# Attention and expert layer on one core: another order of the first quarter on all engines

## The chip, the cores and the metric

The kernel runs on one core of a Trainium2 chip. The metric is the device time of one execution, in microseconds (us). The engines work at the same time, each through its own list of instructions in order: TensorE (PE, with its weight loads PEld), VectorE (DVE), ScalarE (ACT), GpSimd (POOL), and SyncE (SP), which here only issues DMAs.

## The reference

A gated linear attention is followed by a two-layer network with a gated activation. All is float32; B = 4, H = 8 heads, S = 768 steps, D = 48, model width 384, inner width 2048.

```python
f = 1.0 / (1.0 + np.exp(-f_logit))
for t in range(S):
    state = f[:, :, t, :, None] * state + np.einsum('bhd,bhe->bhde', k[:, :, t], v[:, :, t])
    y[:, :, t] = np.einsum('bhd,bhde->bhe', q[:, :, t], state)
x = y.transpose(0, 2, 1, 3).reshape(B * S, H * D)
h = x @ w_in
g = h * np.clip(h + 3.0, 0.0, 6.0) / 6.0
out = g @ w_out
```

## The kernel before, in words

The 768 steps of each of the 4 sequences are cut into 6 chunks of 128. One chunk of one sequence is a *unit*; unit i is sequence i % 4 of chunk i // 4, so there are 24. The four units of a chunk form a *group* of 512 columns for the network, whose inner width is cut into 16 tiles f. A network step is numbered 16 x group + f, so mm1.0 to mm1.15 belong to the first group, which needs units 0 to 3.

The kernel is written as a table, ORDER, of 1,374 small steps, `op.number`, with a third number for the PSUM bank where one is used. A loop walks over the table and issues each step; every engine then gets its own steps in exactly this order, and waits at each for what it reads and for the buffers that it overwrites. Two more tables say which steps go to another engine than their usual one: ON_POOL (to GpSimd instead of VectorE) and ON_ACT (`lim` to ScalarE instead of VectorE).

Steps of a unit:

- `load`, `loadq`, `loadv` (SP): the DMAs of gate logits, of q and k, and of v. `load.i` overwrites the gates that `qmul.i-2` read.
- `gate` (ACT, L368): the sigmoid. Unit 0's is done in two halves, before and after the change.
- `back` (DVE, L375): the scan of the gates backwards; `rend` (L391) its reciprocal, `end` (ACT, L394) a copy; `fwd` (DVE, L399) the scan forwards.
- `kmul` (L388), `qmul` (L404), `decay` (L407): products with k, q and the state, on VectorE or GpSimd.
- `tk` (PE, L462) and `ktok` (ACT, L469): k turned. `kv` (PE, L481), `carry0`, `carry1` (L494 to L503): the new state.
- `att` (PE, L443), `mask` (DVE, L450), `qs` (PE, L513), `av` (PE, L530): the output of the unit, in PSUM.
- `xh` (ACT, L549) takes the output's upper part; `xl` its rest, on VectorE (L562), or, where a `ym` step has first subtracted the upper part on TensorE (L553), as a copy on ScalarE (L560). `hole` (SP, L567, two DMAs) fills the gaps of the layout. Then the unit's columns can be used by `mm1`.

The weights arrive as float64 bit patterns and are turned into a pair of float32 values per tile f: `ld` (SP, L255) loads, `z` (ACT, L278) rounds, `cy` and `lim` (L266, L270 on ACT, or `lim` alone, L272 on DVE) with `mid` (L285), `dif` (L290) and `top` (L294, all DVE) mend the exponent, `high` (ACT, L306) writes the upper part, `low` (L309, or its halves `lowi` and `lowo`) the lower. For tiles 0 to 2 `wd` (SP, L313) keeps the output weights whole.

Network steps: `mm1` (PE, L598, nine matmuls of 512 columns), `relu` (ACT, L608), `g` (DVE, L612), `gh` (ACT, L621), `gl` (DVE or GpSimd, L625), `mm2` (PE, L642). As units 2 and 3 come later than 0 and 1, tiles 0 to 2 of the first group are done in halves of 256 columns: `mm1a`, `relua`, `ga`, `mm2a` need units 0 and 1 alone, `mm1b` and so on units 2 and 3 (L664 to L683). `mm2a` needs `wd`.

`warm.n` is n matmuls on blank data into a bank that nobody reads (L821), `tiny.n` n short ones (L828). They keep TensorE occupied.

A step that writes a PSUM bank waits until every other engine's earlier step on that bank is done. So `att.1` into banks 0 and 1 waits for the steps that read unit 0's output there, and `mm1a.2`, into one of the banks of unit 3's output, waits for `xl.3`. SBUF buffers also turn: three for q and k, three for v, two for gates.

Of the kernel before, what the change touches and what calls it, by code (L numbers as in the profile page):

```python
# [66 lines left out]
loadv.5 top.4 mm2b.0 z.5 carry0.4 relub.1 mid.5 mm2a.2 mask.4 high.4 gb.1 cy.6 carry1.4 dif.5 mm2b.1 low.4 relub.2
lim.6 top.5 tk.5.0 mm1.3.3 z.6 mid.6 fwd.5 mm1.4.4 dif.6 qmul.5 relu.3 gb.2 end.5 high.5 g.3 decay.5 gate.6 low.5
att.5.2 ktok.5 mm2b.2 relu.4 back.6 top.6 qs.4.0 kmul.6 av.4 loadq.7 g.4 high.6 loadv.6 mask.5 loadv.7 mm1.5.4 gh.3
ld.12 lim.7 gh.4 load.7 low.6 ld.11 xh.4 gl.4 ld.15 gl.3 mm2.3 relu.5 rend.6 z.7 g.5 mid.7 z.8 lim.8 mm2.4 dif.7 gh.5  # L70
top.7 z.9 mid.8 mm1.6.2 high.7 dif.8 cy.9 low.7 end.6 top.8 kv.5.0 decay.6 relu.6 tk.6.4 lim.9 mm1.7.3 carry0.5 xl.4
gl.5 cy.10 mid.9 high.8 fwd.6 qs.5.0 relu.7 av.5 dif.9 qmul.6 mm2.5 xh.5 loadv.8 carry1.5 g.7 loadq.8 ktok.6 g.6 z.10
low.8 ym.5 lim.10 mm1.8.4 top.9 gate.7 gh.6 back.7 high.9 att.6.2 mid.10 gh.7 kv.6.0 kmul.7 gl.6 mm2.6 cy.11 rend.7
mask.6 lim.11 dif.10 z.11 low.9 tk.7.2 mm1.9.3 top.10 ktok.7 relu.8 fwd.7 high.10 end.7 relu.9 low.10 gl.7 mm2.7 g.8
carry0.6 gh.8 mm1.10.4 g.9 cy.12 carry1.6 qmul.7 xl.5 mid.11 load.9 gl.8 lim.12 mm2.8 ld.13 decay.7 hole.5 dif.11 gh.9
mid.12 z.12 dif.12 qs.6.2 top.11 att.7.0 loadq.9 top.12 av.6 high.11 load.8 kv.7.0 relu.10 gl.9 mm2.9 low.11 xh.6
carry0.7 mask.7 z.14 g.10 gate.9 qs.7.0 xl.6 z.13 lim.13 av.7 hole.6 mid.13 mm1.11.2 xh.7 lim.14 gh.10 loadv.9 dif.13
hole.4 mid.14 high.12 gl.10 mm2.10 top.13 relu.11 gate.8 g.11 low.12 gh.11 mm1.12.3 high.13 gl.11 carry1.7 xl.7 low.13
hole.7 mm1.13.4 dif.14 loadq.10 top.14 mm2.11 back.8 high.14 relu.12 low.14 kmul.8 z.15 mm1.14.1 lim.15 relu.13 g.12
g.13 mid.15 mm1.16.0 gh.13 dif.15 top.15 gl.13 tk.8.2 high.15 mm2.13 end.8 gh.12 low.15 relu.14 rend.8 gl.12 mm1.15.4  # L80
fwd.8 qmul.8 mm2.12 back.9 relu.15 load.10 relu.16 g.15 ktok.8 g.14 att.8.2 g.16 kv.8.2 gh.14 mm1.17.4 mask.8 gl.14
rend.9 gate.10 fwd.9 gh.15 mm2.14 gl.15 qmul.9 back.10 mm2.15 lowo.0 mm1.19.1 outs.0 outv.1 kmul.9 end.9 gh.16 outs.2
gl.16 decay.8 relu.17 mm1.18.0 od.2 rend.10 load.11 relu.19 g.17 od.0 carry0.8 fwd.10 mm2.16 relu.18 g.19 end.10
qmul.10 carry1.8 g.18 tk.9.3 kmul.10 load.12 lowo.1 mm1.20.4 loadv.10 ktok.9 od.1 gh.17 decay.9 gh.18 gl.17 gate.11
qs.8.0 back.11 att.9.2 decay.10 loadq.11 av.8 kv.9.2 gl.18 xh.8 mm2.17 gate.12 carry0.9 carry1.9 lowo.2 end.11 mask.9
mm1.21.2 gh.19 gl.19 xl.8 tk.10.3 relu.21 mm2.18 ktok.10 g.21 relu.20 rend.11 back.12 qs.9.0 gh.21 fwd.11 att.10.2
# [879 lines left out]
```

## Time and profile before

| | us |
|---|---|
| median of 3 runs | 467.57 (466.38 to 467.74) |
| the profiled execution | 467.04 |
| its span, first to last instruction | 465.3 |
| busy: PE, DVE, ACT, POOL | 453.9, 289.9, 212.3, 63.6 |

A profile row names line, engine, operation, output and inputs, with start and length in us. A part in brackets at its end is the idle time of the engine just before it, and what ended that. In tables of stretches "x" counts instructions; the last three columns are the granted TensorE clock, the DMA engines' busy share and GB/s.

### The profile page before, as it was taken

What the parts mean: (1) busy time and instruction counts of PE and PEld (TensorE: products, weight loads), DVE (VectorE), ACT (ScalarE), POOL (GpSimd) and SP (SyncE); (2) the same over time, 40 slices, a digit from 0 to 9 for tenths busy, and PEclk for the clock granted to TensorE, in tenths of its full rate; (3) what the DMA queues carried; (4) which work ended last, traced back from release to release, by engine and by line L of the source; (5) the groups of instructions that cost most, each with busy time, mean ns of one, the idle gap of its engine ahead of it and who ended that gap; (6) DMA issues with size and microseconds to landing.
All of it is one profiled execution on the core that took longest, in us unless ns stands there. A gap on an engine that the chain in (4) does not pass through costs nothing.

```text
span 465.3 us, 11483 instructions
## 1 busy us (share of the span) xinstructions
PE 453.9 (98%) x4967; PEld 387.4 (83%) x4967; DVE 289.9 (62%) x455; ACT 212.3 (46%) x365; POOL 63.6 (14%) x65
## 2 busy tenths in 40 slices
...
DMA packets 19113, 44.91 MB, mean 97 GB/s; under 512 B 2544, under 2 KB 8816, under 8 KB 19056
## 3 DMA queue, kind: packets, MB, share of 16 engines
...
q8 instruction: 41, 0.67, 0.6%
q10 hardware_dynamic: 288, 0.26, 0.2%
q14 instruction: 16, 0.13, 0.1%
...
## 4 chain that ended last, share of the span: by engine, by line
PE 89%; DVE 3%; ACT 3%; DMA 2%; issue 1%; SPq 0%; POOL 0%; ACTq 0%; POOLq 0%
PE o L642 34%; PE pair L598 25%; PE single L598 12%; PE pair L513 3%; PE pair L530 2%; PE pair L443 2%; PE o L683 2%; PE idle L821 2%; PE pair L481 2%; DMA v<-unit 1%; PE pair L698 1%; PE single L698 1%; PE pair L462 1%; PE pair L664 1%; DVE gg L625 1%
## 5 line engine op out<-in xcount | busy, mean ns | idle before, releaser
L642 PE MATMUL o<-gg,weight 128*128 128x512 f32 x693 | 162.6, 383 | 0.4 <-DVE gg L625 0.3
L642 PEld LDWEIGHTS o<-gg,weight 128*128 128x128 f32 x693 | 129.1, 189 | 19.3 <-DVE gg L625 1.6
L598 PE MATMUL pair<-xts,weight 128*128 128x512 f32 x576 | 133.1, 381 | 0.4 <-DVE tg L612 0.4
L598 PEld LDWEIGHTS pair<-xts,weight 128*128 128x128 f32 x576 | 107.7, 189 | 15.4 <-DVE tg L612 0.8
L625 DVE TENSOR_TENSOR gg<-tg,gg 128x512 fp32r<-128x512 f32 x73 | 54.6, 752 | 56.1 <-ACT gg L621 55.9
L612 DVE SCALAR_TENSOR_TENSOR tg<-tg,pair 128x512 f32<-128x512 f32 x64 | 43.4, 683 | 55.7 <-ACT tg L608 55.5
L608 ACT ACTIVATE tg<-pair,half 128x512 f32<-128x512 f32 x64 | 43.5, 684 | 73.7 <-PE pair L598 68.5
L621 ACT ACTIVATE gg<-tg 128x512 fp32r<-128x512 f32 x77 | 47.7, 627 | 63.9 <-PE o L642 51.1
L598 PE MATMUL single<-xts,weight 128*128 128x512 f32 x261 | 61.9, 382 | 0.0
L598 PEld LDWEIGHTS single<-xts,weight 128*128 128x128 f32 x261 | 48.6, 189 | 6.9 <-DVE tg L612 0.2
L608 ACT ACTIVATE tg<-single,half 128x512 f32<-128x512 f32 x29 | 19.8, 684 | 32.8 <-PE single L598 29.2
L375 DVE TENSOR_TENSOR_SCAN suffix<-gates,unit 112x516 f32<-112x516 f32 (+1 forms) x25 | 29.4, 1180 | 3.4 <-ACT gates L368 3.4
L399 DVE TENSOR_TENSOR_SCAN gates<-gates,rend 112x516 f32<-112x516 f32 x24 | 30.2, 1260 | 0.3
L388 POOL TENSOR_TENSOR qkf<-qkf,suffix 112x512 f32<-112x512 f32 x14 | 20.8, 1483 | 65.9 <-DVE suffix L375 23.1
L612 DVE SCALAR_TENSOR_TENSOR tg<-tg,single 128x512 f32<-128x512 f32 x29 | 19.8, 682 | 9.7 <-ACT tg L608 9.4
L549 ACT ACTIVATE xts<-pair 112x512 fp32r<-112x512 f32 x24 | 14.2, 593 | 24.1 <-PE pair L530 19.4
L407 POOL TENSOR_TENSOR decayed<-state,ends 112x192 f32<-112x192 f32 x13 | 10.2, 786 | 108.6 <-PE pair L513 65.4
L404 POOL TENSOR_TENSOR qkf<-qkf,gates 112x512 f32<-112x512 f32 x11 | 15.8, 1436 | 67.4 <-DVE gates L399 39.3
L642 PE MATMUL o<-xts,weight 128*128 128x512 f32 x96 | 23.4, 380 | 0.0
L450 DVE TENSOR_TENSOR a<-pair,causal 128x512 f32<-128x512 f32 x24 | 16.4, 683 | 8.5 <-PE pair L481 5.3
L625 DVE TENSOR_TENSOR xts<-tg,xts 128x512 fp32r<-128x512 f32 x16 | 10.9, 691 | 15.4 <-ACT xts L621 15.4
L642 PEld LDWEIGHTS o<-xts,weight 128*128 128x128 f32 x96 | 17.6, 190 | 2.3
...
## 6 DMA issues: line engine op xcount, KB each, us to landing
...
xts<-xts SPq DMA_DIRECT2D x48, 48.0 KB, 2.2
weight<-w SPq DMA_DIRECT2D x3, 192.0 KB, 5.1
...
```

Source lines behind the costliest of these rows:

```text
L375: nc.vector.tensor_tensor_scan(flat(sf[:, p])[:, ::-1], gt[:, columns(p)][:, ::-1], flat(unit[:, p])[:, ::-1], 0.0, op0=ALU.mult, op1=ALU.add,
L388: engine("kmul", i).tensor_tensor(parts_of(t, 1), parts_of(t, 1), split(sf[:, :, 1:C + 1]), op=ALU.mult)
L399: nc.vector.tensor_tensor_scan(past, past, flat(rend), 0.0, op0=ALU.mult, op1=ALU.add)
L404: engine("qmul", i).tensor_tensor(parts_of(t, 0), parts_of(t, 0), split(to), op=ALU.mult)
L450: nc.vector.tensor_tensor(d["a"].rearrange("r p e t -> r e p t"), d["at"], causal.unsqueeze(1).unsqueeze(1).broadcast_to([128, 2, NP, HC]) ...
L549: nc.scalar.activation(parts(0), d["y"][:PR], AF.Copy)
L598: nc.tensor.matmul(h, win(f, a, k), turned(g["xt"][:, k, :g["n"] // C, b]), start=i == 0, stop=i == 3 * KT - 1,)
L608: nc.scalar.activation(d["t"], d["h"], AF.Relu, bias=half, scale=1.0 / 6.0)
L612: nc.vector.scalar_tensor_tensor(d["t"], d["t"], 1.0, d["h"], op0=ALU.min, op1=ALU.mult)
L621: nc.scalar.activation(d["gg"][:, 0], d["t"], AF.Copy)
L625: engine("gl", g["first"] + f).tensor_tensor(d["gg"][:, 1], d["t"], d["gg"][:, 0].bitcast(F32), op=ALU.subtract)
L642: nc.tensor.matmul(g["o"][m], wout(f, a, m), halves_of(g[f]["gg"][:, b]), start=f == 0 and i == 0, stop=f == NF - 1 and i == 2, skip_group ...
```

## The change

Only the three tables change. Every engine's list is another one up to about a quarter of the work; from there the lists agree but for a few neighbours. No step's code changes. What the tables say, from the start:

- TensorE: the warm-ups ahead of `tk.0` go from 17 and 8 tiny ones to 14 and 5; over all, from 44 and 8 to 47 and 5 by count of the table. `qs.0` goes ahead of `tk.1`. `ym.0` and `ym.2` are dropped, so `xl.0` and `xl.2` move from ScalarE to VectorE. `mm1a.0` now stands ahead of `kv.3` and `att.3`, `mm1a.1` behind `mm2a.0`, and `att.4`, `kv.4` behind the halves.
- ScalarE: `gate.1` moves behind `ktok.0`; tile 2 is converted ahead of tile 1; `lim.6` and `cy.6` go, `lim.7` and `cy.7` come.
- GpSimd, 48 to 44 steps: `kmul.3`, `kmul.4`, `qmul.5`, `decay.5`, `gl.5`, `gl.14`, `kmul.10` go to VectorE; `qmul.3`, `low.6`, `lowo.1` come from it.
- SP: `loadv.1` behind `load.2`; `ld.2` ahead of `ld.1`; `hole.0`, `hole.1` with `ld.3` ahead of `load.4`, `loadv.3`, `wd.0`, `ld.4`; then `wd.2`, `hole.2`, `ld.5`, `wd.1`, `loadv.4`, `hole.3`.

The core of the diff:

```diff
 ON_POOL = """
-kmul.1 kmul.3 lowi.0 lowi.1 kmul.4 decay.4 kmul.5 qmul.5 decay.5 kmul.6 gl.4 decay.6 gl.5 qmul.6 kmul.7 low.10 low.11
-gl.11 kmul.8 gl.14 qmul.9 lowo.0 kmul.9 decay.8 qmul.10 kmul.10 decay.9 decay.10 lowo.2 kmul.12 decay.12 qmul.13
+kmul.1 lowi.0 qmul.3 lowi.1 decay.4 kmul.5 low.6 gl.4 kmul.6 decay.6 qmul.6 kmul.7 low.10 low.11 gl.11 kmul.8 qmul.9
+lowo.0 kmul.9 decay.8 qmul.10 decay.9 lowo.1 decay.10 lowo.2 kmul.12 decay.12 qmul.13 qmul.14 qmul.15 kmul.15 decay.15
...
 ON_ACT = """
-lim.1 lim.2 lim.4 lim.5 lim.6 lim.9 lim.10 lim.11 lim.12
+lim.2 lim.1 lim.4 lim.5 lim.7 lim.9 lim.10 lim.11 lim.12
 """.split()
 ORDER = """
-load.0 warm.17 tiny.8 loadq.0 load.1 loadv.0 loadv.1 loadq.1 ld.0 gate.0 back.0 rend.0 kmul.0 gate.1 fwd.0 tk.0.0
-end.0 warm.1 ktok.0 qmul.0 kv.0.0 back.1 load.2 att.0.2 carry0.0 ld.1 warm.1 loadq.2 rend.1 kmul.1 mask.0 fwd.1 tk.1.4
-qs.0.0 lim.0 av.0 qmul.1 gate.2 warm.2 end.1 mid.0 ktok.1 load.3 back.2 loadq.3 carry1.0 kv.1.2 xh.0 loadv.2 z.0 ld.2
-warm.9 rend.2 dif.0 loadv.3 fwd.2 cy.1 lim.1 top.0 ym.0 att.1.2 mid.1 gate.3 kmul.2 carry1.1 end.2 qmul.2 xl.0 tk.2.4
-warm.2 carry0.1 mask.1 high.0 wd.0 qs.1.0 back.3 av.1 loadq.4 hole.0 att.2.2 xh.1 dif.1 kmul.3 warm.4 z.1 xl.1 load.4
-mask.2 ktok.2 hole.1 lowi.0 cy.2 rend.3 top.1 tk.3.4 warm.2 ld.3 kv.2.2 ktok.3 lim.2 kv.3.0 fwd.3 carry0.2 z.2 warm.2
-mid.2 qs.2.2 qmul.3 warm.2 carry1.3 dif.2 load.5 att.3.0 gate.4 ld.4 top.2 av.2 high.1 wd.1 mm1a.0.4 loadv.4 carry0.3
-mask.3 lowi.1 end.3 carry1.2 loadq.5 xh.2 back.4 warm.1 high.2 ym.2 qs.3.0 relua.0 av.3 lowi.2 xl.2 kmul.4 lim.3
-warm.1 xh.3 hole.2 mm1a.1.2 ga.0 end.4 xl.3 mm2a.0 relua.1 hole.3 decay.4 gate.5 ga.1 mid.3 z.3 rend.4 mm1a.2.1 dif.3
...
+load.0 warm.14 tiny.5 loadq.0 load.1 loadv.0 loadq.1 ld.0 gate.0 back.0 rend.0 end.0 kmul.0 fwd.0 tk.0.4 warm.3 ktok.0
+gate.1 qmul.0 kv.0.0 back.1 load.2 att.0.2 carry1.0 loadv.1 carry0.0 warm.2 ld.2 rend.1 kmul.1 qs.0.0 loadq.2 mask.0
+fwd.1 tk.1.2 av.0 ktok.1 lim.0 warm.11 xh.0 mid.0 gate.2 qmul.1 z.0 xl.0 load.3 loadv.2 back.2 ld.1 kv.1.2 hole.0
+dif.0 cy.2 att.1.0 top.0 warm.2 loadq.3 lim.2 ld.3 mask.1 end.1 carry0.1 rend.2 z.2 kmul.2 qs.1.0 fwd.2 tk.2.4 gate.3
+warm.2 ktok.2 av.1 qmul.2 warm.4 xh.1 back.3 high.0 att.2.2 cy.1 xl.1 lowi.0 mask.2 hole.1 kv.2.0 lim.1 mid.2 rend.3
+dif.2 carry0.2 load.4 carry1.1 warm.1 qs.2.0 top.2 z.1 loadv.3 wd.0 av.2 mid.1 ld.4 kmul.3 warm.2 xh.2 loadq.4 dif.1 tk.3.3
+fwd.3 mm1a.0.4 ktok.3 high.2 wd.2 top.1 qmul.3 warm.1 xl.2 high.1 kv.3.2 lowi.2 hole.2 relua.0 warm.1 lowi.1 att.3.0
+carry0.3 lim.3 gate.4 warm.2 ga.0 ld.5 end.2 carry1.3 mask.3 wd.1 qs.3.2 cy.4 back.4 loadv.4 av.3 lim.4 warm.2 mid.3
+mm2a.0 kmul.4 end.4 xh.3 decay.4 z.3 xl.3 dif.3 hole.3 mm1a.2.2 z.4 rend.4 mid.4 dif.4 tk.4.3 load.5 relua.2 mm1a.1.4
...
```

47 lines of the change are left out of this document (23 added, 24 removed).

## The prediction

> **What bounds the kernel now.** I read the head of the page first, then a table of stretches, then the chain that ended last, then the rows of each engine in the first 80 us.
>
> ```profile
> PE 453.9 (98%) x4967; PEld 387.4 (83%) x4967; DVE 289.9 (62%) x455; ACT 212.3 (46%) x365; POOL 63.6 (14%) x65
> ```
>
> TensorE is busy for 98% of the span of 465.3, so time can only come from its idle time, its warm-ups, or work that is dropped. Stretch by stretch (length, then busy time of each engine, clock, DMA share):
>
> ```profile
> 3.88:27.62 23.74, 20.75 (x526) 13.08 (x524) 21.98 (x33) 15.81 (x32) 4.16 (x4) 1.00 0.98 339
> 27.62:55.87 28.25, 26.75 (x340) 22.68 (x338) 26.15 (x41) 21.95 (x37) 7.61 (x8) 1.00 0.86 323
> 55.87:77.86 21.99, 21.60 (x249) 17.53 (x247) 21.34 (x33) 21.16 (x29) 7.59 (x6) 1.00 0.49 176
> 110.00:465.30 355.30, 350.04 (x3468) 306.01 (x3467) 188.38 (x298) 130.25 (x233) 34.96 (x29) 1.00 0.18 56
> ```
>
> Until 77.86 us VectorE is as full as TensorE: it idles 1.76, 2.10 and 0.65 us, 4.51 us in all. After 110 us it is busy for 53% and TensorE for 99%: there the order of the small steps decides nothing. The chain shows the hand-over (start, length, what):
>
> ```profile
> 29.84 0.69 PE pair L530 x32
> ...
> 53.82 2.23 PE single L598 x9
> ...
> 56.66 0.87 ACT w L278
> ...
> 71.63 1.60 DVE gg L625
> ...
> 77.92 0.92 PE o L642 x3
> ```
>
> Up to mm1.5 (53.82) the chain is TensorE's; then ScalarE's roundings and VectorE's conversions carry it to gl.7 (ends 77.86); from mm2.7 on it is TensorE's to the end. So the change is worth what it moves two points by: mm1.5 on TensorE, gl.7 on VectorE; the later one counts.
>
> ```profile
> 1.07 5.96 PE L821 MATMUL idle<-blank 128*128 128x512 bf16 x17 [1.07 <-DVE blank L218]
> ...
> 7.07 0.58 PE L462 MATMUL pair<-ident,qkf 112*128 112x112 f32 x4
> ...
> 13.61 2.12 PE L821 MATMUL idle<-blank 128*128 128x512 bf16 x9
> ...
> 33.02 0.38 PE L664 MATMUL pair<-xts,weight 128*128 128x256 f32 x1 [1.28 <-issue]
> 33.23 1.46 PE L683 MATMUL o<-th,weight 128*128 128x256 f32 x6
> ...
> 37.95 1.27 PE L664 MATMUL single<-xts,weight 128*128 128x256 f32 x9
> 39.05 1.17 PE L664 MATMUL pair<-xts,weight 128*128 128x256 f32 x9
> ...
> 73.28 0.92 PE L642 MATMUL o<-gg,weight 128*128 128x512 f32 x3 [0.28 <-DVE gg L625]
> ```
>
> The first output matmul, mm2a.0, starts at 33.23; a half mm1 takes 1.10 (37.95 to 39.05). A warm-up at the full clock takes 0.22 (nine in 2.12, the end of the last apart); the first 17 take 5.96 as the clock is low at the start.
>
> **The change, part by part.** Step lengths on VectorE are differences of starts in this stretch, in which no GpSimd instruction runs:
>
> ```profile
> 7.81 1.23 DVE L375 TENSOR_TENSOR_SCAN suffix<-gates,unit 112x516 f32<-112x516 f32 x1
> ...
> 11.50 0.54 DVE L272 TENSOR_SCALAR y<-raw 128x768 int16<-128x768 int16 x1
> 11.95 0.69 DVE L404 TENSOR_TENSOR qkf<-qkf,gates 112x512 f32<-112x512 f32 x1
> 12.55 0.35 DVE L285 TENSOR_SCALAR t<-y 128x768 int16<-128x768 int16 x1
> 12.82 1.23 DVE L375 TENSOR_TENSOR_SCAN suffix<-gates,unit 112x516 f32<-112x516 f32 x1
> 14.08 0.18 DVE L391 RECIPROCAL rend<-suffix 112x4 f32<-112x4 f32 x1
> 14.18 0.53 DVE L290 TENSOR_TENSOR y<-y,t 128x768 int16<-128x768 int16 x1
> 14.62 1.22 DVE L399 TENSOR_TENSOR_SCAN gates<-gates,rend 112x516 f32<-112x516 f32 x1
> 15.77 1.02 DVE L294 SCALAR_TENSOR_TENSOR w<-y,w 128x768 int16<-128x768 int16 x1
> 16.69 0.33 DVE L285 TENSOR_SCALAR t<-y 128x768 uint16<-128x768 uint16 x1
> 16.95 0.67 DVE L388 TENSOR_TENSOR qkf<-qkf,suffix 112x512 f32<-112x512 f32 x1
> 17.55 0.67 DVE L404 TENSOR_TENSOR qkf<-qkf,gates 112x512 f32<-112x512 f32 x1
> 18.16 0.67 DVE L450 TENSOR_TENSOR a<-pair,causal 128x512 f32<-128x512 f32 x1
> ...
> 33.94 0.42 DVE L678 SCALAR_TENSOR_TENSOR th<-th,pair 128x256 f32<-128x256 f32 x1 [1.38 <-ACT th L673]
> ...
> 71.54 1.69 DVE L625 TENSOR_TENSOR gg<-tg,gg 128x512 fp32r<-128x512 f32 x1
> ```
>
> lim 0.45, a whole 512-wide product or difference (kmul, qmul, mask, xl, gl) 0.60, mid 0.27, back 1.26 (1.14 without the wait for its end), rend 0.10, dif 0.44, fwd 1.15, top 0.92; lowi 0.45 and ga 0.33 by their widths.
>
> *Head.* The warm-ups ahead of tk.0 go from 17 and 8 tiny ones to 14 and 5. The three fall away at the full clock, so tk.0 starts 0.7 earlier than 7.07, at 6.35; kmul.0, two steps ahead of back.1, is done by then. gate.1 moves behind ktok.0 on ScalarE:
>
> ```profile
> 6.54 0.63 ACT L368 ACTIVATE gates<-gates 112x512 f32<-112x512 f32 x1 [2.39 <-DMA gates<-unit]
> ...
> 7.69 0.54 ACT L469 ACTIVATE ktok<-pair 128x448 f32<-128x448 f32 x1 [0.42 <-PE pair L462]
> ```
>
> ktok.0 comes at 6.95, gate.1 at 7.4, so back.1 starts at 8.0 instead of 7.81, 0.2 late; without the earlier tk.0 it would be 0.9. On VectorE then back.1, rend.1, mask.0, fwd.1, lim.0, mid.0, qmul.1, xl.0: 4.91 from 8.0, and 0.6 for fwd.1 behind kmul.1 on GpSimd (below): 13.5. xl.0 is then done, and the ym.0 of before is gone.
>
> *To the first output matmul.* VectorE's list goes on with back.2 to kmul.3: back twice and fwd once (3.67), two dif and two top (2.72), two mid (0.54), rend twice (0.20), six products (3.60): 10.7, kmul.3 done at 24.2. That releases tk.3 and mm1a.0. Then dif.1, fwd.3, top.1, xl.2, lowi.2, lim.3, ga.0, mask.3: 4.94, mask.3 done at 29.1, or 29.7 if the two GpSimd steps beside it (qmul.3, lowi.1) block 0.3 each; I take 29.5. av.3 (0.69, the row at 29.84), two warm-ups (0.43) and the latencies between (0.2) put mm2a.0 at 30.8. The queue of SP now has hole.1 ahead of load.4, loadv.3, wd.0 and ld.4, and hole.1 waits for xl.1 (done at 21.0). Issue to landing:
>
> ```profile
> xts<-xts SPq DMA_DIRECT2D x48, 48.0 KB, 2.2
> weight<-w SPq DMA_DIRECT2D x3, 192.0 KB, 5.1
> ```
>
> wd.0 leaves behind five DMA issues (hole.1 is two) of about 0.5 each, at 23.5, and lands at 28.6, needed at 30.8: covered by 2.2. hole.1 lands at 24.3 in a quiet queue; at wd.0's 5.1 it lands at 27.2 and mm1a.0 slips by 2.6, of which the wait for mask.3 covers all but the ga.0 behind it.
>
> Before, mm1a.1 was already done at mm2a.0; now it isn't. The lead is 33.23 - 30.8 - 1.10 = 1.3 us. From there to mm1.5 the same pieces run in another order, with one new wait: mm1a.2 takes the banks that xl.3 still reads, 0.1 to 0.3. Lead at mm1.5: 1.1.
>
> *What VectorE carries.* Up to gl.7 it gains kmul.3, kmul.4, qmul.5, gl.5, xl.0, xl.2 (0.60 each), decay.5 (0.27) and lim.6 (0.45), 4.32; it loses qmul.3 (0.60), low.6 (0.87, twice lowi's work less its fixed part) and lim.7 (0.45), 1.92. Net 2.4 us more. Against that stand three GpSimd steps fewer in the stretch. What one costs VectorE:
>
> ```profile
> 71.46 1.22 POOL L388 TENSOR_TENSOR qkf<-qkf,suffix 112x512 f32<-112x512 f32 x1 [3.73 <-DVE suffix L375]
> ...
> 77.13 2.43 POOL L309 TENSOR_TENSOR weight<-w,weight 128x768 fp32r<-128x768 f32 x1 [4.45 <-ACT weight L306]
> ```
> ```profile
> L272 DVE TENSOR_SCALAR y<-raw 128x768 int16<-128x768 int16 x7 | 6.6, 937 | 0.0
> ```
>
> gl.6 (71.54) took 1.69 where such a step, product or difference, takes 0.67: it ended 0.6 after kmul.7 on GpSimd did. The lim steps average 0.94 against 0.54 alone. But beside low.10 (77.13, 2.43 long) no step of VectorE was stretched. So between 0 and 1.0 per GpSimd step; I take 0.3, as most rows are unstretched: 0.9 back for three. This agrees in kind with the Trainium skill, "SBUF — State Buffer", "Who interferes with whom": a VectorE instruction with two SBUF inputs and a GpSimd one that reads SBUF lock each other out, and the second to start waits for the whole of the first. By that rule alone three steps of 1.3 would give back up to 3.9 where I take 0.9, and low.6, moved to GpSimd, could take 2.4 of it: gl.7 up to 3.0 earlier or 1.5 later than in my sum, which goes by the 0.3 of the rows.
>
> gl.7 then comes at 77.86 + 2.4 - 0.9 less the idle time saved. Against the 4.51 idle my walk has 0.2 (back.1), 0.6 (fwd.1 behind kmul.1) and 0.5 (ga.2, behind mm1a.2): 3.2 saved, gl.7 at 76.2, 1.7 early. ScalarE loses the copies of xl.0 and xl.2 and is not the limit.
>
> *The sum.* TensorE leads by 1.1 at mm1.5. In 55.87 to 77.86 it idled 0.39, and mm2.6's wait (0.28 at 73.28) belongs to it; with VectorE 1.7 ahead these go: 1.5. The ym.0 and ym.2 that are dropped lay in time that warm-ups filled, nothing. Later swaps (gl.14, kmul.10 to VectorE, lowo.1 to GpSimd) lie where VectorE idles half the time, nothing. The profiled execution took 467.04, 0.5 under the median of the runs, 467.57; 1.5 off its own time is 465.5, off the median 466.1, which is my forecast.
>
> **The rivals.**
> - *VectorE's extra work decides (slower).* If its idle time up to gl.7 stays at 4.5 and the blocking is what it was, gl.7 comes 2.4 later and all behind it: 470.0. It ends slower by 0.3% when idle time and blocking together give back less than 1.0 of the 2.4. For it: VectorE is 97% busy in 55.87 to 77.86. Against: 1.38 of the idle (33.94) is the late mm1a.1, gone by the new order.
> - *The lead is given back (no change).* The 1.28 at 33.02 has no releaser in the trace, so it is in the program before and in none of my steps; if one like it falls between av.3 and mm2a.0, the lead is gone: 467.3.
> - *More.* If neither fwd.1 (0.6) nor the list up to mask.3 (0.4) is blocked, mm2a.0 starts at 29.8, the lead is 33.23 - 29.8 - 1.10 = 2.3, and with the 0.4 of waits at the other end 2.7: 464.9. For it: most rows beside a GpSimd step are unstretched. Against: gl.6 and the mean of lim.
> - *The clock drops.* Three fewer early warm-ups, and a wait for kmul.3 before tk.3. Before, a wait of 1.28 left the granted clock at 1.00. At the start it took some 4.4 us to come up (5.96 less seven warm-ups of 0.22, an estimate); as long at half clock costs 2.2, which makes of the forecast 468.3 and without its gain 469.8. The Trainium skill, "TensorE: Matmul & The Clock Gate", "What's actually happening", gives about 3.4 us of idleness for that; nothing here is near it.
>
> **How the numbers follow.** A difference of 0.3%, 1.4 us, is what a measurement here can tell. The forecast, a gain of 1.0 to 2.2 (465.4 to 466.6), has 0.45, of which 0.35 lies beyond 1.4; the lead given back 0.26; more 0.12; VectorE's extra work 0.14, of which 0.03 within 1.4; the clock 0.03, of which 0.01 within. Faster 0.47, same 0.40, slower 0.13. The range from 463.8 to 468.4 leaves out most of the two slower cases (0.13) and the far end of the gains (0.05).
>
> **What would show it.** Right: tk.0 at 6.35, back.1 at 8.0, mm1a.0 near 24.5, mm2a.0 near 30.8, VectorE's idle between back.0 and gl.7 under 2 us, gl.7 near 76.2, and TensorE without the gap in mm2.6. Wrong: hole.1 landing after 26, a gap without releaser ahead of mm2a.0, VectorE steps of 1 us and more beside qmul.3 and low.6, or TensorE idle behind gl.6 and gl.7 as before.

## The result and the profile after

The changed kernel takes 472.78 us (median of 12 runs, 467.88 to 474.32), the kernel before beside it 467.64 (12 runs, 466.28 to 469.61): a ratio of 1.0097, 95% interval 1.0075 to 1.0119. The change made the kernel 5.1 us slower; 466.1 was forecast, with 468.4 as the upper end. The profiled execution took 472.71 with a span of 470.9, 5.6 over the span before, so the two profiles hold the whole difference of the medians.

Lines of after.py are one less than those of the kernel before (L642 is now L641). First the busy times of the page and its chain by engine; the chain of the kernel before stands as the third row.

```profile
PE 456.1 (97%) x4963; PEld 386.4 (82%) x4963; DVE 296.6 (63%) x461; ACT 211.5 (45%) x363; POOL 59.2 (13%) x61
PE 75%; DVE 11%; DMA 8%; ACT 3%; SPq 1%; issue 1%; DVEq 0%; ACTq 0%
```
```profile
PE 89%; DVE 3%; ACT 3%; DMA 2%; issue 1%; SPq 0%; POOL 0%; ACTq 0%; POOLq 0%
```

TensorE lost its place in the chain to DMAs (2% to 8%) and VectorE (3% to 11%). The same stretches as in the prediction, of the changed kernel, and the stretch to 110 us of the kernel before:

```profile
3.88:27.62 23.74, 20.18 (x446) 12.48 (x445) 21.42 (x33) 14.14 (x26) 2.19 (x2) 0.93 0.84 298
27.62:55.87 28.25, 25.30 (x317) 20.70 (x315) 25.44 (x40) 20.16 (x37) 4.95 (x4) 1.00 0.90 315
55.87:77.86 21.99, 21.84 (x335) 17.22 (x333) 21.85 (x36) 20.12 (x29) 8.94 (x6) 1.00 0.64 242
77.86:110.00 32.14, 30.35 (x317) 24.81 (x315) 30.78 (x46) 21.94 (x34) 7.67 (x4) 1.00 0.27 85
```
```profile
77.86:110.00 32.14, 31.99 (x383) 27.10 (x384) 31.39 (x51) 21.05 (x32) 7.05 (x4) 1.00 0.33 102
```

Three things changed. In the first stretch the clock is 0.93 instead of 1.00 and the DMA share 0.84 instead of 0.98. In the second, VectorE is busy for 0.7 us less although it has more to do: it waits. In the last, where I had put nothing, TensorE is idle for 1.79 us instead of 0.15.

Event by event: gl.7 starts at 80.33 instead of 77.20, 3.1 late; gl.9 ends at 90.35 instead of 85.33, 5.0 late; behind that 0.6 is added, and after 110 us nothing. TensorE's rows (start, length; in brackets the wait and what ended it):

```profile
17.80 0.46 PE L512 MATMUL pair<-qkf,middle 48*64 48x64 f32 x16 [1.86 <-ACT middle L493]
18.19 0.98 PE L461 MATMUL single<-ident,qkf 112*128 112x112 f32 x4
...
19.96 1.13 PE L529 MATMUL pair<-a,v 64*64 64x64 f32 x32
...
34.03 1.56 PE L682 MATMUL o<-th,weight 128*128 128x256 f32 x6
37.02 1.27 PE L663 MATMUL pair<-xts,weight 128*128 128x256 f32 x9 [1.42 <-DVE xts L561]
...
90.41 0.92 PE L641 MATMUL o<-gg,weight 128*128 128x512 f32 x3 [1.20 <-DVE gg L624]
```

*ScalarE's list.* qs.1 (17.80) waits 1.86 us for carry0.1 on ScalarE, and mm1a.2 (37.02) 1.42 for xl.3. Both times ScalarE sat in front of a weight conversion whose DMA had not landed, with the unit's step behind it (for xl.3 there is a second wait, that of kmul.4, below):

```profile
15.42 0.99 ACT L265 ACTIVATE y<-raw,lowest 128x768 uint16<-128x768 int16 x1 [1.77 <-DMA raw<-w]
16.50 0.94 ACT L269 ACTIVATE y<-y,span 128x768 uint16<-128x768 uint16 x1
17.34 0.19 ACT L393 ACTIVATE ends<-suffix 112x4 f32<-112x4 f32 x1
17.44 0.31 ACT L493 ACTIVATE middle<-pair 112x192 f32<-112x192 f32 x1
...
33.70 0.99 ACT L265 ACTIVATE y<-raw,lowest 128x768 uint16<-128x768 int16 x1 [2.34 <-DMA raw<-w]
```

cy.2 waits for ld.2, cy.4 for ld.4; the chain has both transfers, 6.53 us from 8.80 and 7.30 us from 26.38. (It also has two later ones, 8.78 us from 40.27 and 10.38 from 49.07. VectorE's waits there are short, 0.79 us at the most from 47 us to gl.7, so nothing is read into them here.) Behind cy.2 and lim.2 stand end.1 and carry0.1, behind cy.4 stands xh.3.

VectorE has to wait with them, and its rows name the other engine or the DMA each time:

```profile
21.79 0.69 DVE L561 TENSOR_TENSOR xts<-pair,xts 112x512 fp32r<-112x512 f32 x1 [1.35 <-ACT xts L548]
23.06 0.69 DVE L449 TENSOR_TENSOR a<-pair,causal 128x512 f32<-128x512 f32 x1 [0.58 <-PE pair L442]
...
35.45 0.69 DVE L387 TENSOR_TENSOR qkf<-qkf,suffix 112x512 f32<-112x512 f32 x1 [1.36 <-DMA qkf<-unit]
```

These are xl.1, mask.2 and kmul.4; kmul.4 waits for loadq.4, and xl.3 stands right behind it. From 3.88 to the end of gl.7 VectorE is idle for 5.27 us (4.52 before) and busy for 71.84 (69.46 before).

*The clock.* After the 1.86 us without work TensorE is slow: av.1 takes 1.13 where it took 0.69. Stretches of 2 us (the clock is the third number from the right):

```profile
17.00:19.00 2.00, 1.20 (x21) 1.10 (x22) 1.97 (x3) 2.00 (x5) 0.00 (x0) 0.81 1.00 364
19.00:21.00 2.00, 2.00 (x35) 1.04 (x33) 1.44 (x2) 0.61 (x2) 0.00 (x0) 0.50 1.02 377
21.00:23.00 2.00, 2.00 (x56) 1.09 (x56) 0.69 (x1) 1.84 (x3) 0.44 (x1) 0.83 0.51 208
23.00:25.00 2.00, 1.33 (x65) 0.96 (x55) 1.91 (x5) 1.97 (x5) 0.57 (x1) 1.00 0.23 65
```

*SP's list.* Nothing is issued from 16.83 to 22.51, since hole.1 waits there for xl.1; the DMA share falls to 0.51 and 0.23. wd.0 and ld.4 leave behind it:

```profile
16.33 0.50 SPq L254 DMA_DIRECT2D raw<-w  x1
22.51 1.20 SPq L566 DMA_DIRECT2D xts<-xts  x2
23.75 1.51 SPq L350 DMA_DIRECT2D gates<-unit  x1
25.36 0.38 SPq L362 DMA_DIRECT2D v<-unit  x1
25.78 0.55 SPq L312 DMA_DIRECT2D weight<-w  x1
26.38 0.59 SPq L254 DMA_DIRECT2D raw<-w  x1
```

*VectorE beside GpSimd.* lowi.2 and lim.3 are stretched beside two GpSimd steps, qmul.3 and lowi.1, so mask.3 starts at 32.02; and gl.9 is stretched to 2.30, starting 0.41 after low.11. The last two rows are of the kernel before:

```profile
29.54 0.94 DVE L308 TENSOR_TENSOR weight<-w,weight 128x384 fp32r<-128x384 f32 x1
30.40 1.37 DVE L271 TENSOR_SCALAR y<-raw 128x768 int16<-128x768 int16 x1
31.69 0.41 DVE L677 SCALAR_TENSOR_TENSOR th<-th,single 128x256 f32<-128x256 f32 x1
32.02 0.68 DVE L449 TENSOR_TENSOR a<-pair,causal 128x512 f32<-128x512 f32 x1
...
88.05 2.30 DVE L624 TENSOR_TENSOR gg<-tg,gg 128x512 fp32r<-128x512 f32 x1
```
```profile
28.26 1.81 POOL L403 TENSOR_TENSOR qkf<-qkf,gates 112x512 f32<-112x512 f32 x1 [4.69 <-PE single L663]
30.03 1.32 POOL L308 TENSOR_TENSOR weight<-w,weight 128x384 fp32r<-128x384 f32 x1
...
87.64 2.17 POOL L308 TENSOR_TENSOR weight<-w,weight 128x768 fp32r<-128x768 f32 x1 [4.95 <-ACT weight L305]
```
```profile
84.62 0.71 DVE L625 TENSOR_TENSOR gg<-tg,gg 128x512 fp32r<-128x512 f32 x1
84.79 2.24 POOL L309 TENSOR_TENSOR weight<-w,weight 128x768 fp32r<-128x768 f32 x1 [5.22 <-ACT weight L306]
```

Before, gl.9 started 0.17 ahead of low.11 and took 0.71. Both steps are on the same engines in both tables, but their neighbours on VectorE are not in the same order: top.11, for which low.11 waits by way of high.11, now stands ahead of decay.7 and dif.12 instead of behind dif.12. Counted from the start of gl.8, low.11 starts 0.3 us sooner than before (4.13 for 4.41) and gl.9 0.3 later (4.54 for 4.24), and that turns their order round.

### The profile page after: what moved, and what is told of

Read it like the earlier page. It is cut to its first block, busy times and chain, and to the rows that moved or that the text cites. A ratio compares the mean times of both kernels' runs of the same rounds, so it can differ in the third digit from the quotient of the medians.

```text
span 470.9 us, 11461 instructions
## 1 busy us (share of the span) xinstructions
PE 456.1 (97%) x4963; PEld 386.4 (82%) x4963; DVE 296.6 (63%) x461; ACT 211.5 (45%) x363; POOL 59.2 (13%) x61
## 4 chain that ended last, share of the span: by engine, by line
PE 75%; DVE 11%; DMA 8%; ACT 3%; SPq 1%; issue 1%; DVEq 0%; ACTq 0%
PE o L641 31%; PE pair L597 23%; PE single L597 10%; DMA raw<-w 7%; PE pair L512 2%; PE pair L529 2%; DVE w L293 2%; PE pair L442 2%; DVE tg L611 1%; DVE gg L624 1%; PE pair L697 1%; PE single L697 1%; PE pair L480 1%; DVE weight L308 1%; DVE y L289 1%
## 5 line engine op out<-in xcount | busy, mean ns | idle before, releaser
L641 PE MATMUL o<-gg,weight 128*128 128x512 f32 x693 | 162.8, 383 | 1.5 <-DVE gg L624 1.5
L641 PEld LDWEIGHTS o<-gg,weight 128*128 128x128 f32 x693 | 128.7, 189 | 20.9 <-DVE gg L624 2.6
L597 PE MATMUL pair<-xts,weight 128*128 128x512 f32 x585 | 135.9, 382 | 0.6 <-DVE tg L611 0.4
L624 DVE TENSOR_TENSOR gg<-tg,gg 128x512 fp32r<-128x512 f32 x75 | 57.6, 771 | 55.4 <-ACT gg L620 55.2
L597 PE MATMUL single<-xts,weight 128*128 128x512 f32 x252 | 59.9, 383 | 0.0
L597 PEld LDWEIGHTS single<-xts,weight 128*128 128x128 f32 x252 | 46.9, 189 | 6.7 <-DVE weight L308 0.2
L374 DVE TENSOR_TENSOR_SCAN suffix<-gates,unit 112x516 f32<-112x516 f32 (+1 forms) x25 | 30.8, 1235 | 3.3 <-ACT gates L367 3.2
L387 POOL TENSOR_TENSOR qkf<-qkf,suffix 112x512 f32<-112x512 f32 x11 | 16.7, 1515 | 60.5 <-DMA qkf<-unit 30.2
L641 PE MATMUL o<-xts,weight 128*128 128x512 f32 x96 | 23.4, 380 | 0.0
L561 DVE TENSOR_TENSOR xts<-pair,xts 112x512 fp32r<-112x512 f32 x23 | 15.7, 682 | 9.1 <-ACT xts L548 8.9
```

The costliest lines, as they stand in the source:

```text
L374: nc.vector.tensor_tensor_scan(flat(sf[:, p])[:, ::-1], gt[:, columns(p)][:, ::-1], flat(unit[:, p])[:, ::-1], 0.0, op0=ALU.mult, op1=ALU.add,
L387: engine("kmul", i).tensor_tensor(parts_of(t, 1), parts_of(t, 1), split(sf[:, :, 1:C + 1]), op=ALU.mult)
L561: nc.vector.tensor_tensor(parts(1), d["y"][:PR], parts(0).bitcast(F32), op=ALU.subtract)
L597: nc.tensor.matmul(h, win(f, a, k), turned(g["xt"][:, k, :g["n"] // C, b]), start=i == 0, stop=i == 3 * KT - 1,)
L624: engine("gl", g["first"] + f).tensor_tensor(d["gg"][:, 1], d["t"], d["gg"][:, 0].bitcast(F32), op=ALU.subtract)
L641: nc.tensor.matmul(g["o"][m], wout(f, a, m), halves_of(g[f]["gg"][:, b]), start=f == 0 and i == 0, stop=f == NF - 1 and i == 2, skip_group ...
```

## The experiments

Four theories: the clock (A), queue orders on ScalarE and SP (B), VectorE's added work (C), and the late block of gl.9 (D). Each median stands against that of the kernel before, run beside it: 467.65 for e1 to e4, 467.44 for e5 to e8, 466.97 for e9 to e12, 467.36 for e13 to e15 and, for e16, e17 and e18, 467.34, 467.26 and 467.63. The profile of a run is of one execution, which can lie far from the median.

### One cause at a time

```diff
 # e1_warm (A)
-top.0 warm.2 loadq.3
+top.0 warm.10 loadq.3
 # e2_carry (B, ScalarE)
-dif.0 cy.2 att.1.0 ... mask.1 end.1 carry0.1 rend.2
+dif.0 carry0.1 end.1 cy.2 att.1.0 ... mask.1 rend.2
 # e3_hole (B, SP)
-mask.2 hole.1 kv.2.0 ... mid.1 ld.4 kmul.3
+mask.2 kv.2.0 ... mid.1 ld.4 hole.1 kmul.3
 # e4_xh (B, ScalarE)
-cy.4 back.4 loadv.4 av.3 lim.4 ... end.4 xh.3
+back.4 loadv.4 av.3 ... end.4 xh.3 cy.4 lim.4
```

> The changed kernel with eight more warm-ups (2 become 10) ahead of qs.1, where TensorE idled 1.86 us in the changed kernel (start of qs.1 17.80) and the granted clock then fell to 0.50. Theory A, the clock: the fall is what costs, so the clock stays at 1.00 in 15 to 25 us, av.1 takes 0.69 instead of 1.13, hole.1 leaves 1.3 us earlier (21.2 instead of 22.51), and the time falls to 468 +- 1, near the one execution of the changed kernel whose mean clock was 0.999 (467.88). Theory B, the queues: the order on SP (hole.1 ahead of ld.4) and on ScalarE (cy.4 ahead of xh.3) is what costs; the clock gives only its own 1.3, 471.4. Theory C, VectorE's 2.4 us of added work: no change, 472.8.

Measured: 472.26 (469.54 to 473.26, 6 runs), 1.0091 [1.0057, 1.0125]. The profile's clock was 1.00 from 15 to 40 us, av.1 took 0.69, and mm2a.0 came at 33.42 instead of 34.03. By the median the gain is half a microsecond. The profiled execution (471.25) had gl.7 at 78.94, 1.4 sooner than that of the change. By both, most of the 5.1 us stays; filling the gap is not enough.

> The changed kernel with carry0.1 and end.1 ahead of cy.2 on ScalarE, so that carry0.1 no longer stands behind the wait for ld.2's landing (15.42). carry0.1 then starts near 15.0 instead of 17.44, and qs.1 waits only for mask.1 (16.76), TensorE's gap falls from 1.86 to 0.9. Theory A: with so short a gap the clock stays at 1.00, qs.1 comes 1.0 earlier as well, time 467 +- 1. Theory B: some 1.3 to 2.3 us off, 470.5 to 471.5. Theory C: 472.8.

Measured: 471.45 (471.05 to 472.36), 1.0083 [1.0055, 1.0111]. qs.1 came at 16.99, 0.8 sooner, but qs.2 now waited 1.44 (at 24.01) for carry0.2, behind cy.1 in the same list. The clock fell later:

```profile
25.00:28.00 3.00, 3.00 (x37) 2.61 (x29) 2.85 (x4) 1.76 (x3) 1.52 (x1) 0.59 0.79 248
```

One wait mended, the next of the same kind took its place: VectorE's idle time fell from 2.32 to 0.53 us in the stretch to 27.62 and rose from 2.81 to 4.62 in the one behind it.

> The changed kernel with hole.1 behind load.4, loadv.3, wd.0 and ld.4 in SP's queue. ld.4 then leaves near 20.8 instead of 26.38. Theory B: the DMA engines no longer run empty in 21 to 27 (share 0.51, 0.23, 0.52), ld.4 lands by 28 instead of 33.7, cy.4 doesn't hold up xh.3, the gap of 1.42 ahead of mm1a.2 goes, time 469 to 470.5. Theory A: the low clock at 18 to 21.7 stays, most of the loss with it, 472 +- 0.8. Theory C: 472.8. hole.1 itself may land 1 to 2 later behind ld.4's bytes; mm1a.0 has no room for that, but the wait for mask.3 behind it has some 2.

Measured: 473.88 (472.57 to 474.74), 1.0128 [1.0098, 1.0158], by the medians slower than the change itself (the intervals overlap), where theory B expected 469 to 470.5. ld.4 no longer waits behind hole.1, but the small DMAs of hole.1 land among the large ones, and mm1a.0 waits for them:

```profile
30.71 1.85 PE L663 MATMUL single<-xts,weight 128*128 128x256 f32 x9 [3.58 <-DMA xts<-xts]
```

So by the medians hole.1 ahead of ld.4 was the better of two bad orders.

> The changed kernel with cy.4 and lim.4 behind xh.3 on ScalarE. xh.3 then starts near 33.5 instead of 35.67, xl.3 near 34.2 instead of 36.27, and mm1a.2 follows mm2a.0 without its gap of 1.42. Theory B: 1.0 to 1.5 us off, 471.3 to 471.8, unless kmul.4, which waits for loadq.4 until 35.45, holds xl.3 on VectorE, and then under 0.5. Theories A and C: no change, 472.8 +- 0.5.

Measured: 471.86 (471.18 to 472.91), 1.0094 [1.0064, 1.0123]: less than 1 us, not told from nothing. With cy.4 out of the way kmul.4 (36.09) and with it xl.3 (36.70) still waited 1.05 for loadq.4, the last DMA of the same late batch on SP.

> The changed kernel with gl.9 ahead of top.12 on VectorE. In the changed kernel gl.9 started at 88.05, 0.4 after low.11 on GpSimd (87.64, 2.17 long), and took 2.30 instead of 0.68; TensorE then idled 1.20 ahead of the last third of mm2.9. Theory D, the late block: gl.9 now starts at 87.1, ahead of low.11, takes 0.7, the idle time goes, the time falls by 1.0 to 1.4, to 471.4 to 471.8; top.12 may be held up instead, which nobody needs so soon. Theories A and B, which put the loss into the first 40 us: the wait moves elsewhere or was hidden, 472.8 +- 0.4.

```diff
 # e5_gl9 (D)
-top.12 kv.7.0 relu.10 low.11 gl.9 mm2.9
+gl.9 top.12 kv.7.0 relu.10 low.11 mm2.9
```

Measured: 471.63 (469.66 to 474.39, 7 runs), 1.0078 [1.0048, 1.0108]. By the times alone this isn't told from the change. The trace shows the mechanism: gl.9 starts ahead of low.11, takes 0.68, and TensorE is busy for 31.94 of 32.14 where it was 30.35. (In this execution, of 473.69, gl.7 had come at 83.19, 2.9 later than in the change, so its time says nothing of gl.9.)

```profile
89.77 0.68 DVE L624 TENSOR_TENSOR gg<-tg,gg 128x512 fp32r<-128x512 f32 x1
```
```profile
90.46 2.60 POOL L308 TENSOR_TENSOR weight<-w,weight 128x768 fp32r<-128x768 f32 x1 [4.92 <-ACT weight L305]
```
```profile
77.86:110.00 32.14, 31.94 (x357) 27.05 (x355) 31.26 (x51) 23.60 (x35) 9.86 (x5) 1.00 0.28 86
```

### VectorE's added work

e7_map is the kernel before with only the changed choice of engines up to 78 us (kmul.3, kmul.4, qmul.5, decay.5, gl.5 to VectorE, qmul.3 and low.6 to GpSimd); e8_backmap is the changed order with ON_POOL as before.

> The kernel before, its order untouched, with the changed kernel's choice of engine alone, for the steps up to gl.7: kmul.3, kmul.4, qmul.5, decay.5, gl.5 to VectorE, qmul.3 and low.6 to GpSimd. VectorE gains 1.2 us of steps net, and GpSimd has three fewer. Theory C: slower, by 1 to 2: 468.7 to 469.7. The prediction's price of 0.3 us for each GpSimd step beside VectorE: 467.7 + 1.2 - 0.9, 468.0 +- 0.4. By blocking for the whole length: faster, 466.

> The changed order with the choice of engine of the kernel before (kmul.3, kmul.4, qmul.5, decay.5, gl.5, gl.14, kmul.10 back on GpSimd; qmul.3, low.6, lowo.1 back on VectorE). Theory C: 470.8 to 471.8, 1 to 2 below the changed kernel. Theories A and B: no gain, 472.8 +- 0.8, or worse, as GpSimd takes 1.2 to 1.4 for kmul.3 and kmul.4 where VectorE takes 0.67, and tk.3 and tk.4 wait for them.

Measured: e7_map 468.07 (12 runs), 1.0010 [0.9986, 1.0033]; e8_backmap 472.63, 1.0095 [1.0070, 1.0120]. The choice of engines costs 0.5 us of the 5.1 (between -0.7 and 1.5), and taking it back in the changed order gains nothing. So it is not the main cause. It is not all of C, though: by the prediction's prices e7_map has 1.2 of the 2.4 us of added work, as xl.0 and xl.2 stay on ScalarE there.

### Together, and taken apart again

e6_all has the queue orders of e2 and e4, cy.1 and lim.1 behind carry1.1, kmul.4 behind xl.3, gl.9 ahead of top.12, and seven warm-ups more. e15_queues is e6_all without the added warm-ups; e14_warmgl9 the change with gl.9 and warm-ups alone; e10_allwarm e6_all with yet more warm-ups.

```diff
 # e6_all
-att.2.2 cy.1 xl.1 ... kv.2.0 lim.1 mid.2 ... carry1.1 warm.1 qs.2.0
+att.2.2 xl.1 ... kv.2.0 mid.2 ... carry1.1 cy.1 lim.1 warm.4 qs.2.0
-mm2a.0 kmul.4 end.4 ... z.3 xl.3 dif.3
+mm2a.0 end.4 ... z.3 xl.3 kmul.4 dif.3
-top.0 warm.2 loadq.3
+top.0 warm.6 loadq.3
 # e10_allwarm, beyond e6_all (e14_warmgl9 has these too, with warm.10 behind top.0 and warm.4 ahead of qs.2)
-lowi.1 att.3.0 ... qs.3.2
+lowi.1 warm.2 att.3.0 ... qs.3.2 warm.4
```

> The changed kernel with all moves of small steps together: carry0.1 and end.1 ahead of cy.2, carry0.2 and carry1.1 ahead of cy.1, xh.3 ahead of cy.4 (ScalarE), xl.3 ahead of kmul.4 and gl.9 ahead of top.12 (VectorE), and seven more warm-ups over the two gaps ahead of qs.1 and qs.2. Theories B and D: each wait behind a conversion that has not its weights yet goes, mm1a.2 starts near 34.5 instead of 37.02, gl.7 ends near 78.5 instead of 80.99, time 468 to 469.5; clock at 1.00 throughout the first 40 us. Theory C (VectorE's added work): the waits of TensorE come back in 70 to 110 us as VectorE is full there, not below 470.5.

> The kernel of e6_all with two more warm-ups ahead of att.3 and four more ahead of av.3, which fill the gaps of 0.51 and 0.88 us after which the granted clock fell to 0.54 and 0.61 from 33 to 37 us in its profile. Theory of the clock: no fall, mm2a.0 takes 1.56 instead of 2.52, and the time comes to 467.8 to 468.3. Rival, that the fall was free there because VectorE was the bound (mm1a.2 found no gap): 468.8 to 469.3, the clock at 1.00 or not.

> The changed kernel with warm-ups alone (ten instead of two ahead of qs.1, four instead of one ahead of qs.2, two more ahead of att.3, four more ahead of av.3) and gl.9 ahead of top.12; queues as the change has them. Clock theory: as good as e10_allwarm, gl.7 at 78.9 as in e1_warm, span 467 to 468, median 469.0 to 469.8. Queue theory: the queues are worth 1.5 us or more, so 470.5 to 471.5.

> The kernel of e6_all without its added warm-ups (two ahead of qs.1, one ahead of qs.2, as the change has them): queue orders and gl.9 alone. Queue theory: as good as e6_all, 468.8 to 469.6. Clock theory: the clock falls between 18 and 36 us in the profile, and the time is 470 to 471.5.

| | median | ratio to before |
|---|---|---|
| the change | 472.78 | 1.0097 [1.0075, 1.0119] |
| gl.9 alone (e5) | 471.63 | 1.0078 [1.0048, 1.0108] |
| gl.9, warm-ups (e14) | 471.41 | 1.0077 [1.0047, 1.0107] |
| gl.9, queues (e15) | 469.24 | 1.0049 [1.0022, 1.0076] |
| gl.9, queues, warm-ups (e6) | 469.02 | 1.0036 [1.0019, 1.0052] |
| the same, more warm-ups (e10) | 469.34 | 1.0057 [1.0026, 1.0089] |

Read in pairs of medians, the queues are worth 2.1 to 2.4 us and the warm-ups 0.2 at most, as the queue theory expected of e14_warmgl9 and e15_queues. The intervals of each pair overlap; clear of the change is e6_all, which has 3.6 of the 5.1 us back, and e15_queues touches the edge of the change's interval. The one profile of e14_warmgl9 (468.29, gl.7 at 78.67) caught one of its fastest executions and by itself would have spoken for the clock. In e15_queues the clock still fell, and its median is about that of e10_allwarm, in whose profile it did not:

```profile
26.00:30.00 4.00, 4.00 (x62) 3.45 (x61) 4.00 (x6) 2.53 (x5) 2.50 (x2) 0.57 0.86 265
```

That leaves the clock little room by the medians, but it is not settled. Within the runs of one kernel the time goes with the mean clock: of the 12 runs of the change the fastest (467.88) had 0.999, the three slowest (474.06 to 474.32) 0.987 to 0.992. A run with longer waits may have the lower clock because of them, or the other way round; no run here tells which. Against the clock as the cause: the added warm-ups of e14_warmgl9 raised the median of the mean clock from 0.991 (e5_gl9) to 0.996, and the median time fell by 0.2.

### The clock in the kernel before, and the late block there

```diff
 # e12_cold, from the kernel before
-ld.2 warm.9 rend.2
+ld.2 warm.1 rend.2
 # e11_gl6, from the kernel before
-mid.10 gh.7 kv.6.0 kmul.7 gl.6 mm2.6
+gl.6 mid.10 gh.7 kv.6.0 kmul.7 mm2.6
```

> The kernel before with one warm-up instead of nine ahead of tk.1's follower att.1 (from 13.6 us), so that TensorE is idle for about 1.5 us there, as the changed kernel is at 15.9 to 17.8. Theory of the clock: the granted clock falls (0.5 to 0.8 for some us) where it was 1.00, and the time is 1.0 to 2.5 us over the kernel before (468.5 to 470), with a spread between runs of more than 3 us. Rival, that the clock falls in the changed kernel for another reason or costs nothing: 467.3 to 467.8.

Measured: 468.42 (466.30 to 470.02, 12 runs), 1.0029 [1.0003, 1.0055]: 1.4 us by the medians, 0.1 to 2.6 by the interval, as the theory of the clock expected. In its profile TensorE waited 2.19 us ahead of 17.76, and the clock fell after it, yet gl.7 started at 77.12, as early as ever. That execution took 467.30, so it doesn't show where the 1.4 us are lost:

```profile
19.00:21.00 2.00, 1.82 (x75) 1.71 (x68) 1.57 (x2) 0.45 (x1) 0.75 (x1) 0.56 1.02 344
21.00:23.00 2.00, 2.00 (x21) 0.98 (x15) 1.81 (x4) 1.44 (x4) 1.59 (x2) 0.59 0.80 277
```
```profile
77.12 0.65 DVE L625 TENSOR_TENSOR gg<-tg,gg 128x512 fp32r<-128x512 f32 x1
```

> The kernel before with gl.6 ahead of mid.10 on VectorE. There gl.6 started 0.08 us after kmul.7 on GpSimd (71.54 against 71.46) and took 1.69 where its like take 0.7, and TensorE waited 0.28 for it. Theory of the late block (a VectorE tensor step that starts while a GpSimd tensor step runs ends with it): gl.6 takes 0.7 and the wait of 0.28 goes, 467.1 to 467.3 where the kernel before has 467.4 to 467.6. Rival, that the wait is taken up by the next one (blocks limited by VectorE until gl.7): no difference, 467.4 to 467.6.

Measured: 467.24 (12 runs), 1.0011 [0.9982, 1.0041], no difference. The block is gone (gl.6 takes 0.66 at 71.91 instead of 1.69 at 71.54), the wait of 0.28 is gone, and gl.7 comes at 77.16 instead of 77.20: the rival was right, the next wait took it up. This was the one candidate for a version that beats both kernels; it isn't shown to.

### What is left over the kernel before

With the queues and gl.9 mended, 1.6 to 2.4 us are still left. Four tries at it, all from e6_all or e10_allwarm: the old choice of engines (e9_allmap, e13_warmmap), mask.3 sooner (e16_mask3), and the block mm1a.1 back ahead of mm2a.0, alone (e17_mm1a1; its scratch bank is one of the two in which unit 3's output is being summed, so the work is the same but that kernel's output is wrong) or with its whole chain (e18_block).

```diff
 # e16_mask3, from e10_allwarm; qmul.3 is also taken out of ON_POOL
-fwd.3 mm1a.0.4 ktok.3 high.2 wd.2 top.1 qmul.3 ... lowi.2 hole.2 ... warm.2 att.3.0 carry0.3 lim.3 gate.4 warm.2 ga.0 ... mask.3
+fwd.3 qmul.3 mm1a.0.4 ktok.3 high.2 wd.2 top.1 ... hole.2 ... att.3.0 carry0.3 mask.3 ga.0 lowi.2 lim.3 gate.4 warm.2
 # e17_mm1a1 (tk.4.3 becomes tk.4.4)
-qs.3.2 warm.4 ... relua.2 mm1a.1.4
+qs.3.2 mm1a.1.3 ... relua.2
 # e18_block
-av.3 warm.2 mid.3 ... relua.2 mm1a.1.4 ... mm2a.2 relua.1 ld.7 high.3 ga.1 fwd.4 mm2a.1
+av.3 mm1a.1.4 mid.3 ... xh.3 relua.1 cy.4 ... kmul.4 ga.1 dif.3 ... tk.4.3 mm2a.1 ... relua.2 ... mm2a.2 ld.7 high.3 fwd.4
```

> The kernel of e6_all with the engine choice (ON_POOL) of the kernel before: seven steps go back, so VectorE has some 2.4 us less to do before gl.7. In e6_all VectorE was busy for 21.85 of the 21.99 us from 55.87 to 77.86, so the theory that what remains over the kernel before (469.02 against 467.44, 1.6 us) is VectorE's added work expects gl.7 (79.59 in e6_all) at about 78 and a time of 467.4 to 468.0. The rival, that the rest was lost earlier, in the late mask.3 and mm2a.0 (34.60 against 33.23), and that GpSimd's slower steps give back what VectorE saves, expects 468.7 to 469.5.

> The kernel of e10_allwarm with the engine choice of the kernel before. Its profile had gl.7 at 78.44, 1.24 behind the kernel before, with VectorE busy for 21.85 of the 21.99 us ahead of it. Theory that with all waits mended VectorE's added work (2.4 us) is what is left: gl.7 at 77.2 to 77.6, time 467.0 to 468.3 where the kernel before has 467.0 to 467.6. Rival, that GpSimd's slower steps give it back, as e9_allmap (gl.7 78.95, 469.35) showed: gl.7 at 78.4 or later, time 469 to 469.6.

Measured: 469.35, 1.0057 [1.0029, 1.0085], and 470.30, 1.0077 [1.0051, 1.0104]. In e9_allmap gl.7 came at 78.95 (79.59 in e6_all), in e13_warmmap at 79.61 (78.44 in e10_allwarm). No gain; what this says of C stands at the end of this section.

> The kernel of e10_allwarm with qmul.3 on VectorE and ahead of high.2, and mask.3 and ga.0 ahead of lowi.2 and lim.3 (the two warm-ups ahead of att.3 are out again). Theory that the rest of the loss is the late mask.3: mask.3 starts at about 30.0 instead of 31.60, mm2a.0 at about 33.0 instead of 34.60, gl.7 at 77.0 to 77.6 instead of 78.44, time 467.4 to 468.3. Rival, that mm2a.0 isn't on the path and VectorE, with 0.7 us more work, sets gl.7: gl.7 at 78.4 to 79.1, time 469.2 to 469.9.

Measured: 469.52 (469.31 to 469.71, 8 runs), 1.0041 [1.0021, 1.0061]. mask.3 started at 30.59, a microsecond sooner, but qs.3 (31.55) then waited for ScalarE, mm2a.0 came at 34.19, only 0.41 sooner, and gl.7 at 78.80. VectorE was as full ahead of gl.7 as in e10_allwarm:

```profile
55.87:77.86 21.99, 21.90 (x338) 17.91 (x337) 21.85 (x36) 20.36 (x29) 9.05 (x6) 1.00 0.52 191
```

> The kernel of e10_allwarm with the block mm1a.1 (nine matmuls, 1.25 us) moved ahead of av.3, in the place of the four warm-ups there (its scratch bank and that of tk.4 are exchanged for it). Theory that the rest is useful work of TensorE pushed behind the last gaps of the head: gl.7 at 77.2 to 77.7 instead of 78.44, time 467.6 to 468.5. Rival, that VectorE (busy for 21.85 of 21.99 us ahead of gl.7) sets its time and TensorE's block only moves a wait: gl.7 at 78.2 to 78.6, time 469.0 to 469.6.

> The kernel of e10_allwarm with the whole chain of the block in the kernel before's place: mm1a.1 behind av.3 instead of two warm-ups, relua.1 behind xh.3, ga.1 behind kmul.4, mm2a.1 behind tk.4. Theory that the rest over the kernel before is TensorE's useful work pushed behind the head: no wait of 1.2 us or more at 38 to 40, gl.7 at 77.2 to 77.7 (78.44 in e10_allwarm), time 467.6 to 468.5. Rival, that unit 4's steps on VectorE come later by what the block's gate takes, and set gl.7: 78.2 to 79.2 and 469.0 to 469.6.

Measured: 469.21, 1.0053 [1.0030, 1.0076], gl.7 at 79.17; and 471.68, 1.0085 [1.0056, 1.0115], gl.7 at 81.00. The work done sooner came back as waits for VectorE's gate steps, twice in e18_block (0.49 ahead of 40.58, 0.89 ahead of 46.05) and once in e17_mm1a1:

```profile
39.38 2.86 PE L682 MATMUL o<-th,weight 128*128 128x256 f32 x12 [1.52 <-DVE th L677]
```

What the rest is stays open, but the traces narrow it down. From 3.88 us to the end of gl.7:

| | VectorE busy | idle | gl.7 ends |
|---|---|---|---|
| the kernel before | 69.46 | 4.52 | 77.86 |
| the change | 71.84 | 5.27 | 80.99 |
| e15_queues | 71.53 | 3.47 | 78.88 |
| e6_all | 72.14 | 4.25 | 80.27 |
| e10_allwarm | 71.34 | 3.88 | 79.10 |
| e9_allmap | 71.93 | 3.81 | 79.62 |
| e13_warmmap | 72.13 | 4.25 | 80.26 |

With the queues mended VectorE idles no longer than in the kernel before. gl.7 still ends 1.0 to 2.4 us later, because VectorE is busy for 1.9 to 2.7 us more. That is about the 2.4 us of added work, which no run took away in full. e9_allmap and e13_warmmap give back 1.2 of it by the prediction's prices, not the 2.4 that their expectations name, since xl.0 and xl.2 stay on VectorE. Even that does not show in their busy time; GpSimd, with more to do, is busy for 21.7 to 22.0 us there instead of 16.7 to 17.5, and VectorE's steps stretch beside it. Putting ym.0 and ym.2 back, so that xl.0 and xl.2 return to ScalarE, was not tried. So VectorE's longer list is the account that fits the rest, and it is not shown.

## Why the prediction was wrong, point by point

- *Head.* Right. tk.0 started at 6.12 (forecast 6.35), back.1 at 7.83 (8.0), the step behind xl.0 started at 13.38 (13.5); fwd.1 was held 0.4 by kmul.1 (0.6).
- *"To the first output matmul": the first step that failed.* The walk went along VectorE's list alone and took what VectorE reads from the other engines as ready. "ScalarE loses the copies of xl.0 and xl.2 and is not the limit" was true of its busy time and false of its order: cy.2 ahead of carry0.1 put the landing of ld.2 into unit 1's path. qs.1 came at 17.80; xl.1, forecast to be done at 21.0, ended at 22.48, and kmul.3, forecast to be done at 24.2, ended at 26.52. VectorE's waits for xl.1 and mask.2, 1.35 and 0.58, are most of these 2.3 us. e15_queues and e6_all price this term at 2.1 to 2.4 us of the time, together with cy.1, cy.4 and kmul.4.
- *SP.* I costed wd.0 behind hole.1 (to leave at 23.5; it left at 25.78) and hole.1's landing, but not ld.4 and loadq.4, the next in the same queue: ld.4 landed at 33.7, and cy.4 and xh.3 hung on it; kmul.4 hung on loadq.4 (35.45), and xl.3 on both. 1.42 of idle TensorE at 37.02 came of it. The warning sign that I gave, hole.1 landing after 26, was set on the wrong DMA.
- *mask.3.* I allowed 0.4 for blocking by qmul.3 and lowi.1; lowi.2 (0.94 for 0.53) and lim.3 (1.37 for 0.54) gave 1.2. mask.3 ended at 32.70 for 29.5, mm2a.0 started at 34.03 for 30.8: behind the kernel before by 0.8 with mm1a.1 still to do, 1.9 behind instead of 1.3 ahead.
- *What VectorE carries.* The sum for the end of gl.7 was 77.86 + 2.4 - 0.9 - 3.2 = 76.2; it ended at 80.99, which is 77.86 + 2.38 + 0.75. VectorE was busy for 2.38 us more, as much as the added work, so on balance the 0.9 that fewer GpSimd steps should give back did not come. And the "3.2 saved" of its idle time failed outright: it idled 0.75 longer, 5.27 us where the walk had 1.3. So up to gl.7 the rival of VectorE's extra work (idle time as before, nothing given back) came nearest, at a chance of 0.14; what it leaves out are the queue waits that e6_all takes away, and gl.9.
- *"Later swaps ... nothing."* Wrong by 2.5 us for all that lies behind gl.7, by the profiles. I looked only at steps that change engines and at the time behind 110 us, where nothing indeed changed. I left out 77.86 to 110, where VectorE was busy for 31.39 of 32.14 us in the kernel before. There a new order of neighbours put gl.9 behind low.11 (2.30 for 0.71, TensorE idle for 1.20), and TensorE idles 0.15 (102.77) and 0.34 (109.22) more further on. The rule of the Trainium skill that I quoted, "SBUF — State Buffer", "Who interferes with whom", describes gl.9: low.11 ended at 89.81 and gl.9 at 90.35, about its own length later. I had used the rows' mean of 0.3 instead, which says little of a single step: it was held for what was left of the GpSimd step (lowi.2 ended 0.41 behind qmul.3, lim.3 0.42 behind lowi.1), or not at all. Which of two comes first can be told from the rows only where they start some tenths apart. gl.7 started 0.07 and 0.08 behind low.10 in the two traces and took 0.66 both times, while gl.6, 0.08 behind kmul.7 in the kernel before, took 1.69.
- *The clock.* I gave it 0.03, by the 3.4 us of idleness that the Trainium skill names ("TensorE: Matmul & The Clock Gate", "What's actually happening"). Here a wait of 1.86 was followed by 0.50, and the 1.28 of the kernel before was not; the measurement decides. Nor does the length of one wait settle it, as the last section shows. As a cause it looks small, since warm-ups gained 0.2 to 0.5 by the medians, but it isn't excluded: a forced fall cost the kernel before 1.4 [0.1, 2.6].

The sum of the difference by the two profiles: 3.1 up to gl.7, 1.9 at gl.9 and 0.6 behind it. By the medians: the queues, with the clock that falls beside them, 2.1 to 2.4; gl.9 about 1, which the times alone don't tell from nothing; and 1.6 to 2.4 open.
